# Regrouping gradients by a mask and four matmuls, and a shorter tail of the norm's backward, in a two-layer decode step with its backward

## The chip, the cores and the metric

The kernel runs on one core of a Trainium2 chip. The metric is the device time of one execution in microseconds; of several executions the median is given. Everything below is about one kernel before and one after the change.

## What is computed

Two layers, each an attention block over a long key and value cache and an MLP, with the gradients of the output with respect to all nine inputs. Cut to what matters:

```python
def _A_ref(x, k_cache, v_cache, wq, wo):          # x: 2 x 1 x 1024, caches: 2 x 4 x 16384 x 128
    q = (x @ wq).reshape(B, Sq, Hq, Dh)           # 32 heads of 128, 8 to each of 4 cached heads
    p = softmax(q @ k^T * Dh ** -0.5)
    return (p @ v) @ wo

def _B_ref(x, w1, b1, w2, b2):
    y = _layernorm(x, axis=-1)
    h = _gelu(y @ w1 + b1)                        # F = 3584
    return h @ w2 + b2

x = A_x
for layer in (0, 1):
    x = x + _A_ref(_layernorm(x), k_cache, v_cache, wq, wo)
    x = x + _B_ref(_layernorm(x), w1, b1, w2, b2) # _B_ref norms once more
out, vjp = jax.vjp(f, A_x, k_cache, v_cache, wq, wo, w1, b1, w2, b2)
grads = vjp(grad_out)                             # out and nine gradients are returned
```

There are two batch rows and a single query position, so every activation is a vector of 1024 (or 3584, or 4096) for each of two rows, while the caches and the weights are tens of megabytes that are read several times. The gradients of the caches and the weights are outer products of such vectors and are written in full.

## The kernel before

A vector lives in SBUF as a tile of 128 partitions by `DJ` = 8 columns by 2 batch rows (`[128, DJ, 2]`): element `j * 128 + p` stands in partition `p`, column `j`. The work goes through these stages: forward attention of layer 0, its MLP, forward attention of layer 1, its MLP together with the backward of that MLP, backward attention of layer 1 (`attn_bwd(1, ...)`), backward of layer 0's MLP, and backward attention of layer 0 (`attn_bwd(0, ...)`), in which nearly all gradients of weights and caches are also formed and written.

Every piece of work is a Python function handed to `emit`, with the chunks it uses. `Program.run` then walks the pieces in order; the order of instructions on each engine is the order of the pieces, and nothing is moved afterwards. Loads come from SyncE's queue into slots of 1 MB (`slot0` to `slot15` and parts of other tiles); a load is given a slot, and issued, as early as a slot is free whose use ends in time. In the last stage part of the slots becomes staging for outputs, which GpSimd's queue stores.

Two sides work on copies out of PSUM: `copy_bf` and `cast_out` choose between ScalarE and VectorE (DVE) by a running account of how busy each is, `st["act"]` and `st["dve"]`; pieces with fixed DVE work book it with `dve(...)`. PSUM banks for short uses come in rotation from `ob()`, three of them in most of the backward.

For weights that were only transposed in blocks of 32 (`turn_rows`, `turned_products`), a product comes out in what is called quad layout here: `acc[p, c, a, b]`, where partition block `p // 32` and the index `a` have changed places against the layout that the next step needs. `unquad` sets that right: DVE copies the PSUM region to the tile `uq`, and 16 copies of 32 partitions each move the blocks, dealt out to DVE, ScalarE and GpSimd in turn (lines L517, L525, L527, L529). It is used in seven places: `g3_` (gradient of layer 1's MLP input, `dm_1`), `g1p` (the same of layer 0, `dm_0`), three times in `wo_bwd_ops` (gradient of the attention's output in layer 0, `do_raw`, one for each cached head after the first, followed by `do_of`), `dh_last_` and `dn_kept`; the last two put all copies on GpSimd.

The backward of a norm is three helpers. `ln_bwd_terms` makes the two sums over columns (`lb_s`), `part_sum` sums them over partitions by a matmul with ones (L594), and `ln_bwd_rest` makes the gradient. Behind the partition sums these DVE operations follow one another: a scaling of the sums by -1/1024 (`lb_nm`, L665), for the MLP a second scaling (L667), three operations on `lb_u` (L669 to L671), the product with `rstd` (`lb_dx`, L673), the addition of the other gradient (L936 or L1191) and, where the next products need it, a cast to bf16 (L937 or L1194). `mlp_in_bwd` calls them for the MLP's input, `attn_in_bwd` for the attention's input; in `attn_in_bwd` the three parts `sums`, `close` and `rest` are pieces of their own.

`do_of` (L1002 to L1008) takes the regrouped gradient, spreads it for the next products (L563, L566) and sums it over partitions. `exchange` (L585) is the set of 16 copies, on ScalarE or GpSimd, that the backward attention needs for each half head. `kblock` transposes a block of a cache on DVE (L537) and uses it on TensorE (L550); `direct` (L575) uses it untransposed. L1266 and L1326 are the products of the outputs' gradients, L276 and L279 the casts of these to bf16 on ScalarE and DVE.

Of the kernel before, what the change touches and what calls it, by code (L numbers as in the profile page):

```python
# [182 lines left out]
def kernel(  # L183
# [113 lines left out]
    for w in range(2):  # L297
        for e in range(2):
            V.tensor_copy(out=selp[:, 2 * w + e],
                          in_=ident[:].rearrange("p (w t e) -> p w e t", w=2, e=2)[:, w, e].unsqueeze(1).to_broadcast(  # L300
                              [128, 4, 32]))
    neghalf = const.tile([128, 2], F32, name="neghalf")
# [349 lines left out]
    def ln_bwd_terms(dy, y):  # L652
        t1 = wrk.tile([128, DJ, 2], F32, name="lb_t1")
        V.tensor_tensor(out=t1[:], in0=dy, in1=y, op=ALU.mult)
        s = small.tile([128, 2, 2], F32, name="lb_s")
        V.tensor_reduce(out=s[:, 0, :], in_=dy.rearrange("p j b -> p b j"), axis=AX.X, op=ALU.add)
        V.tensor_reduce(out=s[:, 1, :], in_=t1[:].rearrange("p j b -> p b j"), axis=AX.X, op=ALU.add)
        return flat(s[:])

    def ln_bwd_sums(dy, y, at=None):  # L660
        return part_sum(ln_bwd_terms(dy, y), 4, at)

    def ln_bwd_rest(ps, dy, y, rstd, twice=False):
        nm = small.tile([128, 2, 2], F32, name="lb_nm")
        V.tensor_scalar(out=flat(nm[:]), in0=ps, scalar1=-1.0 / D, scalar2=None, op0=ALU.mult)  # L665
# [257 lines left out]
    def mlp_in_bwd(l, fill, gT, parts=False):  # L923
        h = {}

        def sums():
            y, _ = saved[f"m{l}"]
            h["dm"] = wrk.tile([128, DJ, 2], F32, name="dm_sb")
            fill(h["dm"])
            h["ps"] = ln_bwd_sums(h["dm"][:], y[:], half[0, 0] if parts else None)  # L930

        def rest():
            y, r = saved[f"m{l}"]
            dx = ln_bwd_rest(h["ps"], h["dm"][:], y[:], r[:], True)
            gn = vec.tile([128, DJ, 2], F32, name=f"gM{l}")
            V.tensor_tensor(out=gn[:], in0=dx[:], in1=gT[:], op=ALU.add)  # L936
            V.tensor_copy(out=gA_all[:, :, 2 * l:2 * l + 2], in_=gn[:])  # L937
# [23 lines left out]
    def wo_bwd_ops(l, k, vb):  # L961
# [3 lines left out]
        def fin():  # L965
            raw = small.tile([128, 8, 2], F32, name="do_raw")
            unquad(raw[:].rearrange("p (c j) b -> p c j b", j=4), acc)
            V.memset(sb[0][:, 64:80], 0.0)
            dve(1.1)
            do_of(l, k, raw[:])  # L970
# [200 lines left out]
    def attn_in_bwd(l, gT, dnq):  # L1171
        h = {}

        def sums():
            dn = wrk.tile([128, DJ, 2], F32, name="dn")
            last = sb[0][:, 112:128].rearrange("p (j b) -> p j b", b=2)
            if l == 1:
                V.tensor_copy(out=dn[:], in_=last)
            else:
                V.tensor_tensor(out=dn[:], in0=last, in1=dnq[:], op=ALU.add)  # L1180
            h["dn"] = dn
            h["s"] = ln_bwd_terms(dn[:], vec_y[f"a{l}"][:])
            dve(0.8)

        def close():
            h["ps"] = part_sum(h["s"], 4, half[0, 0] if l == 1 else sb[0][:, 200:])

        def rest():
            dx = ln_bwd_rest(h["ps"], h["dn"][:], vec_y[f"a{l}"][:], vec_r[f"a{l}"][:])
            gn = saved[f"gA{l}"]  # L1190
            V.tensor_tensor(out=gn[:], in0=dx[:], in1=gT()[:], op=ALU.add)  # L1191
            dve(1.3)
            if l == 1:
                V.tensor_copy(out=gM_all[:, :, 0:2], in_=gn[:])  # L1194
# [295 lines left out]
    def g3_():  # L1490
        saved["g3"] = mlp_in_bwd(1, lambda dm: unquad(dm[:].rearrange("p (c j) b -> p c j b", j=4), dm_1), gT4)
# [57 lines left out]
    g1p = mlp_in_bwd(0, lambda dm: unquad(dm[:].rearrange("p (c j) b -> p c j b", j=4), dm_0), g2, parts=True)  # L1549
# [97 lines left out]
```

## Time and profile before

| | us |
|---|---|
| median of 3 runs | 1108.54 |
| lowest and highest of them | 1106.45, 1108.61 |
| the profiled execution | 1104.69 |
| its span | 1102.9 |
| TensorE matmuls busy | 809.1 (73% of the span) |
| DVE busy | 759.6 (69%) |
| ScalarE busy | 492.6 (45%) |
| GpSimd busy | 181.7 (16%) |
| bytes moved by DMA | 448.98 MB, mean 407 GB/s |

The profile is of one execution. Engines are called PE (TensorE's matmuls), PEld (its weight loads), DVE, ACT (ScalarE), POOL (GpSimd) and SP (SyncE, which only issues DMAs here). A row of the timeline has the start in us from the span's start, the length in us, engine, line, operation, what it writes and reads, the form, the count and, in brackets, how long the engine had stood idle and what ended that. A row of the groups has busy us, mean ns of one, and idle us before. A row of the windows has the busy time and count of PE, PEld, DVE, ACT and POOL in a stretch, the clock granted to TensorE as a share of full speed, the DMA engines' mean busy share and the rate in GB/s. Idle time of an engine that does not bound a stage costs nothing.

### The profile page before, as it was taken

To read this page: it belongs to the slowest core of one execution; us is meant where nothing else is said; L and a number is where in the kernel's file an instruction comes from. 1 tells how busy PE (TensorE), PEld (TensorE's weight loads), DVE (VectorE), ACT (ScalarE), POOL (GpSimd) and SP (SyncE) were. 2 spreads that over 40 slices of the span, in tenths; PEclk is the share of its full clock that TensorE was granted. 3 is DMA by queue.
4 is the path that set the end of the run, shared out by engine and by line. 5 is a ranking of instruction groups with operands and counts; after the bars stand their busy time and mean duration, and the time that the engine had idled before them with its cause. 6 is when DMAs were issued, how large, how long until landed. Compare 5 with 4: busy or idle time off the path is not lost. (4 is left out here: it accounts for less than half of the span.)

```text
span 1102.9 us, 34164 instructions
## 1 busy us (share of the span) xinstructions
PE 809.1 (73%) x14665; PEld 607.6 (55%) x14677; DVE 759.6 (69%) x1472; ACT 492.6 (45%) x1133; POOL 181.7 (16%) x575
## 2 busy tenths in 40 slices
PE   5665666457788657688778678878876986598795
PEld 4554565456777556688778564444443443344453
DVE  5864665168888637755746466979876896598974
ACT  0332222101242321235534326767675776477874
POOL 1000000001000000111211101433332332233330
PEclk9999999999999999988978657989997999799998
DMA  9999999999999999999999998999999999999996
GB/s 372 420 423 421 421 425 423 397 385 413 416 422 421 422 420 383 419 418 421 416 421 419 389 413 307 366 400 424 419 420 425 423 419 422 425 411 420 411 423 269
DMA packets 97932, 448.98 MB, mean 407 GB/s; under 512 B 7624, under 2 KB 11742, under 8 KB 59380
## 3 DMA queue, kind: packets, MB, share of 16 engines
q1 hardware_dynamic: 80532, 351.32, 78.2%
q0 software_dynamic: 17248, 95.48, 21.0%
q8 instruction: 115, 1.88, 0.6%
q14 instruction: 37, 0.30, 0.1%
HBM read 348.15 MB, written 98.62 MB: 405 GB/s over the span
## 5 line engine op out<-in xcount | busy, mean ns | idle before, releaser
L537 DVE STREAM_TRANSPOSE kT<-slot 128x512 int32<-128x512 int32 x436 | 294.1, 695 | 109.5 <-PE sc L550 90.9
L550 PE MATMUL sc<-qbd,kT 128*128 128x32 bf16 x4096 | 263.0, 222 | 11.0 <-DVE kT L537 10.2
L550 PEld LDWEIGHTS <-kT 128*128 128x128 bf16 x4096 | 209.1, 115 | 65.3 <-issue 33.4
L575 PEld LDWEIGHTS <-slot 128*128 128x128 bf16 x3456 | 141.9, 103 | 101.4 <-issue 45.3
L575 PE MATMUL sb<-xt,slot 128*128 128x8 bf16 x3456 | 157.6, 177 | 45.7 <-DMA slot<-in_A_v_cache_dram 23.9
L276 ACT CAST slot<-sc 128x512 bf16<-128x512 f32 x281 | 160.8, 594 | 58.2 <-PE sc L1326 25.0
L1266 PE MATMUL sc<-slot,late 128*128 128x512 bf16 x344 | 127.8, 392 | 23.3 <-DVE slot L279 10.0
L279 DVE CAST slot<-sc 128x512 bf16<-128x512 f32 x172 | 115.2, 678 | 24.5 <-PE sc L1326 10.4
L768 ACT ACTIVATE e<-sc 128x512 bf16<-128x512 f32 x32 | 19.0, 597 | 234.8 <-DVE sc L765 168.6
L276 ACT CAST slot<-sb 128x512 bf16<-128x512 f32 x151 | 89.6, 593 | 37.0 <-PE sb L1326 25.3
L455 ACT COPY slot<-tp 128x512 int32<-128x512 int32 x88 | 50.4, 587 | 106.0 <-PE tp L452 90.3
L452 PE MATMUL tp<-ident,slot 128*128 128x128 bf16 x768 | 74.4, 260 | 11.0 <-DMA slot<-in_A_wq_dram 5.7
L585 ACT COPY xt<-e 32x128 int32<-32x128 int32 x256 | 75.6, 295 | 3.9
L1266 PEld LDWEIGHTS <-late 128*128 128x128 bf16 x512 | 44.5, 98 | 59.5 <-issue 45.7
L1266 PE MATMUL sb<-slot,late 128*128 128x512 bf16 x162 | 63.7, 393 | 7.6 <-DVE slot L279 1.9
L1326 PE MATMUL sc<-slot,late 128*128 128x512 bf16 x155 | 58.7, 401 | 13.8 <-DVE slot L279 9.9
L452 PEld LDWEIGHTS <-slot 128*128 128x128 bf16 x768 | 60.1, 119 | 13.6 <-issue 6.3
L437 DVE STREAM_TRANSPOSE slot<-slot 128x1024 int32<-128x1024 int32 (+1 forms) x46 | 52.9, 1178 | 18.6 <-DMA slot<-in_A_wo_dram 9.1
L279 DVE CAST slot<-sb 128x512 bf16<-128x512 f32 x80 | 54.1, 677 | 9.5 <-PE sb L1266 6.2
L645 POOL TENSOR_TENSOR m_rstd<-ln_vpe,neghalf 128x2 f32<-128x2 f32 x2 | 1.4, 719 | 349.0 <-DVE ln_vpe L643 349.0
L585 POOL COPY xt<-late 32x64 int32<-32x64 int32 x240 | 55.6, 232 | 13.0 <-DVE late L1054 1.9
L585 POOL COPY xt<-ds 32x64 int32<-32x64 int32 x128 | 29.7, 232 | 148.5 <-DVE ds L1054 113.9
(298 smaller groups left out, 1090.9 us busy)
## 6 DMA issues: line engine op xcount, KB each, us to landing
slot<-in_A_k_cache_dram SPq DMA_DIRECT2D x103, 1024.0 KB, 16.4
slot<-in_A_v_cache_dram SPq DMA_DIRECT2D x101, 1024.0 KB, 16.0
out_dram<-slot POOLq DMA_DIRECT2D x55, 1024.0 KB, 14.3
slot<-in_A_wq_dram SPq DMA_DIRECT2D x25, 1024.0 KB, 12.4
slot<-in_A_wo_dram SPq DMA_DIRECT2D x25, 1024.0 KB, 19.7
out_dram<-slot POOLq DMA_DIRECT2D x40, 512.0 KB, 14.1
slot<-in_B_w_dram SPq DMA_DIRECT2D x22, 896.0 KB, 16.4
slot<-in_B_w_dram SPq DMA_DIRECT2D x12, 1024.0 KB, 12.8
```

The costliest lines, as they stand in the source:

```text
L276: S.copy(out=dst, in_=src)
L279: V.tensor_copy(out=dst, in_=src)
L437: V.transpose(out=t.ap[:, h * nw * 256:(h + 1) * nw * 256].bitcast(I32).rearrange("p (w j m) -> p w j m", j=4, m=32), in_=c.ap[:, 0:4 * nc ...
L452: PE.transpose(tp[:, j * 128:(j + 1) * 128], c.ap[:, off + j * 128:off + (j + 1) * 128], ident[:])
L455: S.copy(out=d.bitcast(I32), in_=tp.bitcast(I32))
L537: V.transpose(out=kT[:].bitcast(I32).rearrange("p (w j m) -> p w j m", w=4, j=4), in_=c.ap[:, (i % 4) * 1024:(i % 4 + 1) * 1024].bitcast(I ...
L550: PE.matmul(sc[:, a0:a0 + 4, :, 2 * (i % 4) + q], lhsT=kv[:, 2 * q + w, :, e], rhs=qbd[:, q_at(g), 2 * w + e], start=(w == 0 and e == 0), ...
L575: PE.matmul(acc, lhsT=c.ap[:, n * 128:(n + 1) * 128], rhs=xv[:, i // 4, t // 2, :, 2 * (i % 4) + t % 2], start=(fresh and i == 0 and t == ...
L585: (GP.tensor_copy if on[t % len(on)] == "g" else S.copy)(out=d[32 * t:32 * t + 32, c0:c0 + cn, j, :], in_=s[32 * j:32 * j + 32, c0:c0 + cn ...
L768: S.activation(out=e_of(l, g)[:, 8 * f:8 * f + 8].rearrange("p a h b -> p h a b"), in_=sc[f][:].rearrange("p h (a b) -> p h a b", b=8), fu ...
L1266: PE.matmul(ps, lhsT=hold["blk"][:, j, :], rhs=flat(qm(w)[:, hf * 4:hf * 4 + 4, :]), start=True, stop=True)
L1326: PE.matmul(ps, lhsT=hold[j // 4 * 4][:, j % 4, :], rhs=Y.ap[:, y_at + c0:y_at + c0 + cn], start=True, stop=True)
```

## The change

`regroup` takes the place of `unquad` in `mlp_in_bwd` (both layers) and in `wo_bwd_ops`. It multiplies the PSUM region, with `a` spread over four columns, by a mask that keeps a partition's own block, and then sums blocks by four fp32 matmuls with a matrix of 128 x 32 ones at equal remainders; each writes 32 partitions of a PSUM bank. The result is read from PSUM by what follows; there is no copy to SBUF. `dh_last_` and `dn_kept` keep `unquad`.

In the norm's backward the product with `rstd` is made first, on the incoming gradient (`lb_dr`); the scalings go into the matrix of the partition sum (`mean`, -1/1024 in place of ones) and into the product in front of it; the other gradient is added to `lb_dr` between the partition sum's matmul and what reads it. Behind the sums stay a product, an addition and a last addition that is written directly, once for each form that is needed (bf16 for the products first, fp32 second). The account of DVE work is booked with 0.3 in place of 1.1 in the `do` step and 0.8 in place of 1.3 in `attn_in_bwd`.

```diff
+    quadT = vec.tile([128, 32], F32, name="quadT")
+    V.tensor_reduce(out=quadT[:], in_=identf[:].rearrange("p (a t) -> p t a", a=4), axis=AX.X, op=ALU.add)
+    mean = vec.tile([128, 1], F32, name="mean")
+    V.memset(mean[:], -1.0 / 1024)
+    meanf = mean[:].to_broadcast([128, 128])
...
+    def regroup(src, at):
+
+        C = src.shape[1]
+        q = small.tile([128, 8, 4, 2], F32, name="uq", bufs=1)[:, 0:4 * C]
+        V.tensor_tensor(out=q, in0=src.rearrange("p c a b -> p (c a) b").unsqueeze(2).to_broadcast([128, 4 * C, 4, 2]),
+                        in1=quad[:].unsqueeze(1).unsqueeze(3).to_broadcast([128, 4 * C, 4, 2]), op=ALU.mult)
+        ps = at[:, 0:8 * C].rearrange("p (c n) -> p c n", c=C)
+        qa = q.rearrange("p (c a) j b -> p c a (j b)", a=4)
+        for a in range(4):
+            PE.matmul(ps[32 * a:32 * a + 32], lhsT=quadT[:], rhs=qa[:, :, a], start=True, stop=True)
+        return ps.rearrange("p c (j b) -> p (c j) b", b=2)
...
-    def ln_bwd_terms(dy, y):
+    def ln_bwd_terms(dy, y, rstd, gT, twice=False):
+
+        dr = wrk.tile([128, DJ, 2], F32, name="lb_dr")
+        V.tensor_tensor(out=dr[:], in0=dy, in1=bcast_j(rstd, DJ), op=ALU.mult)
         t1 = wrk.tile([128, DJ, 2], F32, name="lb_t1")
-        V.tensor_tensor(out=t1[:], in0=dy, in1=y, op=ALU.mult)
+        V.scalar_tensor_tensor(out=t1[:], in0=dr[:], scalar=1.0 + LN_EPS if twice else 1.0, in1=y, op0=ALU.mult, op1=ALU.mult)
...
-    def ln_bwd_rest(ps, dy, y, rstd, twice=False):
-        nm = small.tile([128, 2, 2], F32, name="lb_nm")
-        V.tensor_scalar(out=flat(nm[:]), in0=ps, scalar1=-1.0 / D, scalar2=None, op0=ALU.mult)
-        if twice:
-            V.tensor_scalar(out=nm[:, 1, :], in0=nm[:, 1, :], scalar1=1.0 + LN_EPS, scalar2=None, op0=ALU.mult)
+        return dr, flat(s[:]), gT
+
+    def ln_bwd_sums(dr, s, gT, at=None):
+
+        ps = (ob() if at is None else at)[:, 0:4]
+        PE.matmul(ps, lhsT=meanf, rhs=s, start=True, stop=True)
+        V.tensor_tensor(out=dr[:], in0=dr[:], in1=gT, op=ALU.add)
+        return ps
+
+    def ln_bwd_rest(ps, dr, y, outs):
+
         u = wrk.tile([128, DJ, 2], F32, name="lb_u")
-        V.tensor_tensor(out=u[:], in0=y, in1=bcast_j(nm[:, 1, :], DJ), op=ALU.mult)
-        V.tensor_tensor(out=u[:], in0=u[:], in1=dy, op=ALU.add)
-        V.tensor_tensor(out=u[:], in0=u[:], in1=bcast_j(nm[:, 0, :], DJ), op=ALU.add)
-        dx = wrk.tile([128, DJ, 2], F32, name="lb_dx")
-        V.tensor_tensor(out=dx[:], in0=u[:], in1=bcast_j(rstd, DJ), op=ALU.mult)
-        return dx
+        V.tensor_tensor(out=u[:], in0=y, in1=bcast_j(ps[:, 2:4], DJ), op=ALU.mult)
+        V.tensor_tensor(out=u[:], in0=u[:], in1=dr[:], op=ALU.add)
+        for out in outs:
+            V.tensor_tensor(out=out, in0=u[:], in1=bcast_j(ps[:, 0:2], DJ), op=ALU.add)
...
         def sums():
-            y, _ = saved[f"m{l}"]
-            h["dm"] = wrk.tile([128, DJ, 2], F32, name="dm_sb")
-            fill(h["dm"])
-            h["ps"] = ln_bwd_sums(h["dm"][:], y[:], half[0, 0] if parts else None)
+            y, r = saved[f"m{l}"]
+            dm = regroup(src, half[0, 1] if parts else ob())
+            h["dr"], s, g = ln_bwd_terms(dm, y[:], r[:], gT[:], True)
+            h["ps"] = ln_bwd_sums(h["dr"], s, g, half[0, 0] if parts else None)
 
         def rest():
             y, r = saved[f"m{l}"]
-            dx = ln_bwd_rest(h["ps"], h["dm"][:], y[:], r[:], True)
             gn = vec.tile([128, DJ, 2], F32, name=f"gM{l}")
-            V.tensor_tensor(out=gn[:], in0=dx[:], in1=gT[:], op=ALU.add)
-            V.tensor_copy(out=gA_all[:, :, 2 * l:2 * l + 2], in_=gn[:])
+            ln_bwd_rest(h["ps"], h["dr"], y[:], [gA_all[:, :, 2 * l:2 * l + 2], gn[:]])
             return gn
...
         def fin():
-            raw = small.tile([128, 8, 2], F32, name="do_raw")
-            unquad(raw[:].rearrange("p (c j) b -> p c j b", j=4), acc)
+            raw = regroup(acc, ob())
             V.memset(sb[0][:, 64:80], 0.0)
-            dve(1.1)
-            do_of(l, k, raw[:])
+            dve(0.3)
+            do_of(l, k, raw)
...
         def close():
-            h["ps"] = part_sum(h["s"], 4, half[0, 0] if l == 1 else sb[0][:, 200:])
+            h["ps"] = ln_bwd_sums(h["dr"], h["s"], h["g"], half[0, 0] if l == 1 else sb[0][:, 200:])
 
         def rest():
-            dx = ln_bwd_rest(h["ps"], h["dn"][:], vec_y[f"a{l}"][:], vec_r[f"a{l}"][:])
             gn = saved[f"gA{l}"]
-            V.tensor_tensor(out=gn[:], in0=dx[:], in1=gT()[:], op=ALU.add)
-            dve(1.3)
-            if l == 1:
-                V.tensor_copy(out=gM_all[:, :, 0:2], in_=gn[:])
+            ln_bwd_rest(h["ps"], h["dr"], vec_y[f"a{l}"][:], ([gM_all[:, :, 0:2]] if l == 1 else []) + [gn[:]])
+            dve(0.8)
```

In `attn_in_bwd` the part `sums` calls `ln_bwd_terms` with `rstd` and the other gradient; in layer 1 it reads its input from PSUM where it was copied to SBUF before.

More of the change, by code (lines that the diff above doesn't have):

```diff
@@ L1174, in sums @@
         def sums():
-            dn = wrk.tile([128, DJ, 2], F32, name="dn")
             last = sb[0][:, 112:128].rearrange("p (j b) -> p j b", b=2)
-            if l == 1:
-                V.tensor_copy(out=dn[:], in_=last)
-            else:
+            if l == 0:
+                dn = wrk.tile([128, DJ, 2], F32, name="dn")
                 V.tensor_tensor(out=dn[:], in0=last, in1=dnq[:], op=ALU.add)
-            h["dn"] = dn
-            h["s"] = ln_bwd_terms(dn[:], vec_y[f"a{l}"][:])
+                last = dn[:]
+            h["dr"], h["s"], h["g"] = ln_bwd_terms(last, vec_y[f"a{l}"][:], vec_r[f"a{l}"][:], gT()[:])
             dve(0.8)
         def close():
-            h["ps"] = part_sum(h["s"], 4, half[0, 0] if l == 1 else sb[0][:, 200:])
+            h["ps"] = ln_bwd_sums(h["dr"], h["s"], h["g"], half[0, 0] if l == 1 else sb[0][:, 200:])
         def rest():
-            dx = ln_bwd_rest(h["ps"], h["dn"][:], vec_y[f"a{l}"][:], vec_r[f"a{l}"][:])
             gn = saved[f"gA{l}"]
-            V.tensor_tensor(out=gn[:], in0=dx[:], in1=gT()[:], op=ALU.add)
-            dve(1.3)
-            if l == 1:
-                V.tensor_copy(out=gM_all[:, :, 0:2], in_=gn[:])
+            ln_bwd_rest(h["ps"], h["dr"], vec_y[f"a{l}"][:], ([gM_all[:, :, 0:2]] if l == 1 else []) + [gn[:]])
+            dve(0.8)
         res = [(sums, ()), (close, ()), (rest, ())]
@@ L1490, in g3_ @@
     def g3_():
-        saved["g3"] = mlp_in_bwd(1, lambda dm: unquad(dm[:].rearrange("p (c j) b -> p c j b", j=4), dm_1), gT4)
+        saved["g3"] = mlp_in_bwd(1, dm_1, gT4)
     emit(g3_)
@@ L1548 @@
     va0, spread_a0 = spread(lambda: gA_all[:, :, 0:2], DJ, "va")
-    g1p = mlp_in_bwd(0, lambda dm: unquad(dm[:].rearrange("p (c j) b -> p c j b", j=4), dm_0), g2, parts=True)
+    g1p = mlp_in_bwd(0, dm_0, g2, parts=True)
     emit(g1p[0])
```

7 lines of the change are left out of this document (2 added, 5 removed).

## The prediction

> **What bounds the kernel now.** I read the page first, for the span and the slices, then the windows for the two places where the slices dip, then SyncE's timeline and the waits for what ends those dips, and last the timeline around each step that changes. The profiled execution took 1104.69 us; its span is
>
> ```profile
> span 1102.9 us, 34164 instructions
> GB/s 372 420 423 421 421 425 423 397 385 413 416 422 421 422 420 383 419 418 421 416 421 419 389 413 307 366 400 424 419 420 425 423 419 422 425 411 420 411 423 269
> ```
>
> so 1.8 us lie around it. The transfer rate stands near 420 GB/s almost everywhere and dips at slice 25 (662 to 689 us) and in the last one. The windows (columns: the five engines' busy time with counts, granted clock, DMA share, GB/s) say how deep:
>
> ```profile
> 677.00:680.00 3.00, 2.62 (x32) 1.34 (x31) 0.98 (x2) 3.00 (x8) 0.00 (x0) 1.00 0.01 3
> 680.00:683.00 3.00, 2.85 (x37) 1.60 (x34) 2.26 (x4) 3.00 (x9) 0.57 (x1) 1.00 0.45 49
> 683.00:686.00 3.00, 2.68 (x24) 1.08 (x22) 2.87 (x6) 2.38 (x6) 0.71 (x1) 1.00 0.92 328
> 730.00:1080.00 350.00, 283.06 (x3449) 153.99 (x3457) 276.41 (x476) 243.55 (x489) 118.74 (x349) 0.93 1.02 420
> 1080.00:1094.00 14.00, 10.49 (x107) 4.98 (x105) 10.61 (x26) 10.44 (x19) 2.15 (x4) 1.00 0.84 336
> ```
>
> From 730 to 1080 the DMA engines are never free (share 1.02, 420 GB/s); from 677 to 683 they stand still for 2.97 + 1.65 = 4.6 us; from 1080 to 1094 they are idle for 0.16 x 14 = 2.2 us (by the rates, 336 against 420, 2.8 us). Bytes do not change, so time can only be won where DMA idles. What ends the first dip is the issue of loads on SyncE:
>
> ```profile
> 659.42 0.38 SPq L378 DMA_DIRECT2D slot<-in_A_wo_dram  x1
> 669.31 0.33 SPq L373 DMA_DIRECT2D slot<-in_A_v_cache_dram  x1
> 680.98 0.33 SPq L373 DMA_DIRECT2D slot<-in_A_k_cache_dram  x1
> ```
>
> One load in 21 us: all slots are full until the last backward attention begins to use them up, and it begins behind the gradient step of layer 0's MLP (`g1p`). Before that, the compute waited on loads to the end of the second layer's backward attention:
>
> ```profile
> 635.42 0.93 PEld L575 LDWEIGHTS <-slot 128*128 128x128 bf16 x32 [3.55 <-DMA slot<-in_A_k_cache_dram]
> ```
>
> Here TensorE stood 3.55 us for a load. So whatever an earlier step wins (the first use of the new regrouping, `g3_`, stands ahead of that attention) is waited away by 635; I cost it at nothing, covered by that wait, and if the cover were gone it would bring about what the same step brings at 662, below. From 635 to the dip the chain is compute, and a microsecond won there is a microsecond less of idle DMA.
>
> **The change part by part.** I name the layers by their index, 1 and 0. Seven steps used `unquad`; five of them now regroup by a mask and matmuls (MLP gradients of both layers, three `do` steps of layer 0). The two with all copies on GpSimd stay.
>
> *The regrouping itself.* It replaces one copy and 16 small copies on three engines by a DVE product of 64 columns and four fp32 matmuls with 32 output rows. Nearest rows, the product first:
>
> ```profile
> L891 DVE TENSOR_TENSOR g_a<-hpre 128x56 f32<-128x56 f32 x2 | 0.4, 218 | 0.1
> ```
>
> 0.22 us, or 0.24 at 64 columns, and 0.06 to the next engine. For the matmuls no row has this form. An fp32 matmul shows as two weight loads and two matmuls, and the one of the MLP step in question, with 128 weight columns, stands so:
>
> ```profile
> 664.32 0.50 PEld L594 LDWEIGHTS sc<-lb_s,one 128*128 128x128 f32 x2 [2.68 <-DVE lb_s L657]
> 664.32 0.59 PE L594 MATMUL sc<-lb_s,one 128*128 128x4 f32 x2 [2.18 <-DVE lb_s L657]
> ...
> 664.95 0.16 DVE L665 TENSOR_SCALAR lb_nm<-sc 128x4 f32<-128x4 f32 x1 [0.68 <-PE sc L594]
> ```
>
> 0.63 us to its reader, 0.50 of it weight loads. Four such in series would be 2.5 us: the upper end. One of them is the lower end, 0.63. A weight load of few fp32 columns is shorter:
>
> ```profile
> L1370 PEld LDWEIGHTS sc<-identf,g_a 128*36 128x36 f32 x1 | 0.1, 97 | 0.6 <-DVE g_a L1368 0.6
> ```
>
> 97 ns at 36 columns, so eight of them 0.78 us and 0.13 us until the reader: 0.9 us, the value I take, since 36 columns are nearest to 32. With the product the regrouping takes 1.2 us (0.9 to 2.8).
> A row of the other narrow form, 64 output columns amid full ones, shows no gap around it:
>
> ```profile
> 673.13 0.64 PE L1247 MATMUL tp<-ident,e 128*64 128x128 bf16 x8
> ```
>
> The rule against the change is in the Trainium skill, "TensorEngine Tiling", Key Properties: changing the tiling mode drains TensorE, and four 32-column matmuls between full-width ones change it twice. By the row above the drain is invisible and the sum stays; if each drain cost one matmul's length of the fence before (0.59 / 2 = 0.3 us), each regrouping would take 0.6 us more and the forecast's gain would be 2.6 us in place of 3.2.
>
> *Layer 0's MLP step.* DVE alone, from the copy to the first operation of the norm's backward:
>
> ```profile
> 661.74 0.17 DVE L517 COPY uq<-sb 128x16 f32<-128x16 f32 x1 [1.49 <-PE sb L487]
> 661.95 1.03 DVE L525 COPY dm_sb<-uq 32x4 f32<-32x4 f32 x6
> 663.89 0.17 DVE L654 TENSOR_TENSOR lb_t<-dm_sb,m_y 128x16 f32<-128x16 f32 x1 [0.91 <-ACT dm_sb L527]
> ```
>
> 2.15 us, 0.91 of it a wait for ScalarE's share of the copies; 0.43 us later, at 664.32, the sums' matmul starts. After: 1.2 for the regrouping, one operation more in front of the sums (0.2), 0.43: 1.8 in place of 2.58, a gain of 0.7 us (a loss of 0.9 to a gain of 1.0). What is late next is not the norm's tail: behind the sums' matmul TensorE's queue holds six output matmuls, and only then the products that need the gradient, at
>
> ```profile
> 667.39 1.89 PE L465 MATMUL sb<-gA_all,slot 128*128 128x2 bf16 x64
> ```
>
> 2.4 us after the norm's first operation behind the sums (664.95); these six hide the shortened tail, so I count it at nothing here. The new wait: TensorE stands for DVE's product before the four matmuls, and queued behind it are these same six; they waited for the sums before, which came later.
>
> *Layer 1's attention norm, just before.* No regrouping, but the tail is on the path, since TensorE has nothing but the products behind it:
>
> ```profile
> 640.02 0.16 DVE L665 TENSOR_SCALAR lb_nm<-sc 128x4 f32<-128x4 f32 x1 [0.68 <-PE sc L594]
> ...
> 641.26 0.17 DVE L1194 CAST gM_all<-gA 128x16 bf16<-128x16 f32 x1
> ```
>
> Seven operations, 0.21 apart, end at 641.43: 1.41 us. Three remain (0.6): a gain of 0.8 us, 0.5 if each of the two that now read PSUM took 0.15 more. In front of the sums the count is unchanged (a copy goes, a product comes). The addition of the other gradient moves beside the sums' matmul (0.63) and is hidden by it.
>
> Together the dip ends 1.5 us earlier (a loss of 0.4 to a gain of 1.9).
>
> *The three `do` steps of layer 0.* The last of them:
>
> ```profile
> 953.13 0.17 DVE L517 COPY uq<-sb 128x16 f32<-128x16 f32 x1
> 953.33 1.14 DVE L525 COPY do_raw<-uq 32x4 f32<-32x4 f32 x6
> 954.48 0.07 DVE L968 MEMSET sb<- 128x16 f32 x1
> 957.04 0.17 DVE L1002 TENSOR_TENSOR dof<-do_raw,rbc 128x16 f32<-128x16 f32 x1 [2.50 <-POOL do_raw L529]
> ...
> 957.48 0.28 PE L563 MATMUL sb<-qd,selp 128*128 128x16 bf16 x4 [4.76 <-DVE qd L1003]
> ```
>
> 3.91 us, of which 2.50 waits for GpSimd, whose queue has `exchange` copies and a store's issue in front of its five copies. After: 1.2 us, a gain of 2.7 (1.1 to 3.0); GpSimd's store issues are no longer behind five copies. For the first two such steps I count nothing: DMA is saturated, and compute runs into late weights anyway:
>
> ```profile
> DVE slot L437 <- DMA slot<-in_A_wo_dram: 9.1, 2, 5.0
> ```
>
> (waits from 820 to 945). After 957 the only wait for a transfer is half a microsecond:
>
> ```profile
> DVE slot L279 <- DMA out_dram<-slot: 0.5, 1, 0.5
> ```
>
> So from the third step on compute runs free to the end, 2.7 us ahead; but it can win only what DMA idles in the last stretch, 2.2 us. I take 1.7, between nothing and all of it and nearer to the cap because the gain exceeds the cap; it is not all, because the last stores keep their own time from issue to landing. The final norm loses one DVE operation net (0.2 us), inside that.
>
> *The planner.* The new step books less DVE time, and in the built programs five casts of 512 columns go from ScalarE to DVE and four shorter copies the other way:
>
> ```profile
> L279 DVE CAST slot<-sc 128x512 bf16<-128x512 f32 x172 | 115.2, 678 | 24.5 <-PE sc L1326 10.4
> L525 DVE COPY do_raw<-uq 32x4 f32<-32x4 f32 x18 | 3.2, 178 | 0.3
> ```
>
> 5 x 0.678 = 3.4 us come, 3.2 us of small copies go, in the same stage: even. The order of loads on SyncE's queue is the same in both programs.
>
> Sum: 1.5 + 1.7 = 3.2 us; 1104.69 - 3.2 = 1101.5 for an execution like the profiled one. The median of the runs, 1108.54, lies 3.85 above it, so the forecast is 1108.54 - 3.2 = **1105.3**.
>
> **The rivals.** *Compute sets the end and the clock stays up.* In the do step TensorE stood 4.76 us, and behind it
>
> ```profile
> 957.00:963.00 6.00, 4.50 (x37) 2.42 (x39) 1.71 (x7) 3.34 (x7) 0.01 (x1) 0.50 1.02 426
> ```
>
> it worked 4.50 us at a granted clock of 0.50: at full clock 2.2 us less. If the shorter stand keeps the clock up and the last stores don't hold the end, the gain is 1.5 + 2.7 + 2.2 = 6.4 us, 1102.1. Against it: DMA's 1.02 share. The Trainium skill, "TensorE: Matmul & The Clock Gate", What's actually happening, has the clock halved after an idle window of about 3.4 us; the 4.76 us and the 0.50 agree.
>
> *Nothing that lasts.* The regrouping costs its upper 2.8 us, the MLP step loses 0.9 in place of winning, and the tail's idle is the stores' own: 0 to 2.2 us, about 1107.5. For it: no row has these matmuls.
>
> *Slower: weights behind stores.* Between the `do` steps compute runs faster, issues stores earlier, and these share the DMA engines with the weights and values that layer 0's steps at 922 to 941 us wait for. A store of 1 MB is 2.5 us at 420 GB/s. Three stores ahead delay the landing by 7.5; less 2.7 and 1.5 the end comes 3.3 us later, 1111.8. It decides from 6.4 us of delay on, two to three stores. For it: the waits of 5.0 us exist. Against it: stores ahead are also stores done.
>
> *The change does nothing of what it says:* the built program has one product and four matmuls in each of the five places and 80 copies fewer; no chance.
>
> **How the numbers follow.** A measurement tells about 0.2%, 2.2 us, from no change. Forecast 0.45 (its own range 1104.4 to 1106.3, wins of 2.2 to 4.1), the larger gain 0.13, nothing that lasts 0.25, slower 0.17: faster 0.58, same 0.25, slower 0.17. The range runs from 1101.0, below the larger gain, to 1110.0, over the second rival and the bounds of the runs; the third lies outside.
>
> **What would show it.** Right: in the changed profile the MLP step takes 1.8 us from the product to the sums' matmul; the load of 680.98 comes 1.5 us earlier and 677 to 683 idles about 3 us; DVE's wait for GpSimd in the `do` steps is gone, the product to `dof` takes 1.2 us, and 957 to 963 has a clock over 0.9. Wrong: four matmuls of over 2 us; an unchanged dip; longer waits for `wo` than 9.1 us; a last stretch that idles its 2.2 us as before.

## The result, and the profile after

| | before | after |
|---|---|---|
| median, us (22 runs each) | 1106.38 | 1104.51 |
| lowest, highest | 1105.24, 1109.65 | 1103.18, 1107.48 |
| profiled execution, us (span) | 1104.69 (1102.9) | 1103.3 (1101.5) |

The ratio after to before is 0.9981 (95% interval 0.9974 to 0.9988): 2.1 us less, between 1.3 and 2.9. The forecast was 3.2 less.

The changed kernel's windows (the same columns as before: five engines' busy time with counts, granted clock, DMA share, GB/s):

```profile
677.00:680.00 3.00, 2.88 (x39) 1.77 (x37) 1.42 (x2) 3.00 (x8) 0.40 (x1) 0.94 0.03 11
680.00:683.00 3.00, 2.70 (x24) 1.21 (x23) 2.61 (x5) 2.76 (x6) 0.51 (x2) 1.00 0.74 164
730.00:1080.00 350.00, 288.17 (x3463) 154.67 (x3462) 275.65 (x459) 240.00 (x475) 115.90 (x334) 0.92 1.01 421
1080.00:1094.00 14.00, 9.40 (x96) 4.39 (x94) 9.61 (x23) 8.97 (x16) 2.18 (x4) 0.99 0.79 310
957.00:963.00 6.00, 5.95 (x42) 2.43 (x41) 4.55 (x7) 3.48 (x8) 1.27 (x2) 0.69 1.02 429
```

From 677 to 683 DMA idles 2.9 + 0.8 = 3.7 us where it idled 4.6. From 1080 to 1094 it idles 0.21 x 14 = 2.9 us where it idled 2.2: no gain at the end. SyncE's timeline says when the loads around the dip are issued:

```profile
659.66 0.38 SPq L383 DMA_DIRECT2D slot<-in_A_wo_dram  x1
668.26 0.33 SPq L378 DMA_DIRECT2D slot<-in_A_v_cache_dram  x1
679.70 0.33 SPq L378 DMA_DIRECT2D slot<-in_A_k_cache_dram  x1
```

The load of 680.98 comes at 679.70. The MLP step of layer 0, in the changed kernel's timeline:

```profile
661.98 0.22 DVE L540 TENSOR_TENSOR uq<-sb,quad 128x64 f32<-128x64 f32 x1 [1.49 <-PE sb L492]
662.32 0.31 PE L545 MATMUL sc<-uq,quadT 128*32 128x16 f32 x8
662.69 0.18 DVE L672 TENSOR_TENSOR lb_dr<-sc,m_rstd 128x16 f32<-128x16 f32 x1 [0.49 <-PE sc L545]
663.34 0.59 PE L683 MATMUL sc<-lb_s,mean 128*128 128x4 f32 x2 [0.71 <-DVE lb_s L677]
664.38 0.17 DVE L693 TENSOR_TENSOR gA_all<-lb_u,sc 128x16 bf16<-128x16 f32 x1
666.40 1.83 PE L470 MATMUL sb<-gA_all,slot 128*128 128x2 bf16 x64
```

The regrouping takes 0.71 us to its reader, the step 1.36 us to the sums' matmul. The third `do` step, DVE's product to `dof`, takes 0.59 us, where it took 3.91:

```profile
951.79 0.21 DVE L540 TENSOR_TENSOR uq<-sb,quad 128x64 f32<-128x64 f32 x1
952.06 0.26 PE L545 MATMUL sb<-uq,quadT 128*32 128x16 f32 x8
952.38 0.17 DVE L1018 TENSOR_TENSOR dof<-sb,rbc 128x16 f32<-128x16 f32 x1 [0.23 <-PE sb L545]
```

Behind it, from 957 us on, stand waits for transfers, the longest of them below, that the kernel before did not have (it waited 0.5 us):

```profile
POOL out_dram L1287 <- DMA out_dram<-slot: 9.7, 2, 6.5
ACT e L276 <- DMA out_dram<-e: 4.5, 1, 4.5
DVE e L279 <- DMA out_dram<-e: 2.4, 1, 2.4
```

Layer 1's attention norm: the products that need its result start earlier behind the norm, and stop in mid-batch until the same time. The last K load's wait and the two parts of the batch, first of the changed kernel:

```profile
635.66 0.93 PEld L592 LDWEIGHTS <-slot 128*128 128x128 bf16 x32 [2.31 <-DMA slot<-in_A_k_cache_dram]
640.88 5.76 PE L470 MATMUL sb<-gM_all,slot 128*128 128x2 bf16 x211 [0.67 <-DVE gM_all L693]
649.17 0.49 PE L470 MATMUL sb<-gM_all,slot 128*128 128x2 bf16 x13 [2.52 <-issue]
```

and of the kernel before:

```profile
641.49 5.98 PE L465 MATMUL sb<-gM_all,slot 128*128 128x2 bf16 x219 [1.51 <-DVE gM_all L1194]
649.15 0.27 PE L465 MATMUL sb<-gM_all,slot 128*128 128x2 bf16 x5 [1.68 <-issue]
```

The batch has 224 products. TensorE stands 1.68 us in one kernel and 2.52 in the other, "issue" being time in which it waited for nothing that the profile shows, and goes on at 649.15 and 649.17.

### The profile page after: what moved, and what is told of

Read it like the earlier page. It is cut to its first block, busy times and chain, and to the rows that moved or that the text cites. A ratio compares the mean times of both kernels' runs of the same rounds, so it can differ in the third digit from the quotient of the medians.

```text
span 1101.5 us, 34179 instructions
## 1 busy us (share of the span) xinstructions
PE 814.9 (74%) x14717; PEld 608.0 (55%) x14717; DVE 756.1 (69%) x1438; ACT 486.1 (44%) x1107; POOL 177.0 (16%) x550
## 3 DMA queue, kind: packets, MB, share of 16 engines
q8 instruction: 115, 1.88, 0.6%
## 5 line engine op out<-in xcount | busy, mean ns | idle before, releaser
L276 ACT CAST slot<-sc 128x512 bf16<-128x512 f32 x288 | 163.9, 593 | 78.9 <-PE sc L1337 43.5
L1277 PE MATMUL sc<-slot,late 128*128 128x512 bf16 x338 | 127.4, 398 | 29.8 <-DVE slot L279 13.4
L279 DVE CAST slot<-sc 128x512 bf16<-128x512 f32 x168 | 112.8, 678 | 25.1 <-PE sc L1277 13.1
L276 ACT CAST slot<-sb 128x512 bf16<-128x512 f32 x137 | 81.1, 592 | 22.3 <-PE sb L1337 9.6
L1277 PEld LDWEIGHTS <-late 128*128 128x128 bf16 x512 | 44.9, 99 | 64.4 <-issue 51.7
L457 PE MATMUL tp<-ident,slot 128*128 128x128 bf16 x768 | 71.4, 253 | 9.5 <-DMA slot<-in_A_wq_dram 5.2
L1337 PE MATMUL sc<-slot,late 128*128 128x512 bf16 x169 | 65.7, 407 | 16.3 <-DVE slot L279 8.4
L1277 PE MATMUL sb<-slot,late 128*128 128x512 bf16 x174 | 69.7, 400 | 9.6 <-DVE slot L279 4.2
L279 DVE CAST slot<-sb 128x512 bf16<-128x512 f32 x91 | 61.8, 679 | 14.1 <-PE sb L1277 6.9
L602 POOL COPY xt<-ds 32x64 int32<-32x64 int32 x128 | 29.7, 232 | 176.8 <-DVE ds L1070 107.4
## 6 DMA issues: line engine op xcount, KB each, us to landing
slot<-in_B_w_dram SPq DMA_DIRECT2D x22, 896.0 KB, 16.6
```

The costliest lines, as they stand in the source:

```text
L276: S.copy(out=dst, in_=src)
L279: V.tensor_copy(out=dst, in_=src)
L457: PE.transpose(tp[:, j * 128:(j + 1) * 128], c.ap[:, off + j * 128:off + (j + 1) * 128], ident[:])
L602: (GP.tensor_copy if on[t % len(on)] == "g" else S.copy)(out=d[32 * t:32 * t + 32, c0:c0 + cn, j, :], in_=s[32 * j:32 * j + 32, c0:c0 + cn ...
L1277: PE.matmul(ps, lhsT=hold["blk"][:, j, :], rhs=flat(qm(w)[:, hf * 4:hf * 4 + 4, :]), start=True, stop=True)
L1337: PE.matmul(ps, lhsT=hold[j // 4 * 4][:, j % 4, :], rhs=Y.ap[:, y_at + c0:y_at + c0 + cn], start=True, stop=True)
```

## The experiments

The edits below are cut to the lines that matter. The profiled executions take 653 to 658 us to move the first 60 in 100 of their bytes, also where their programs are alike to there, so I compare stretches. The first table is worked out from the transfers' records of each profiled execution: the time between the moments at which 60, 65, 80 and 98 in 100 of its 449 MB had been moved, and the end of the last transfer. The dip lies between 60 and 65.

| kernel | to 60 | 60 to 65 | 65 to 80 | 80 to 98 | 98 to end | 80 to end |
|---|---|---|---|---|---|---|
| before | 653.5 | 64.4 | 160.9 | 193.2 | 29.4 | 222.6 |
| norm_only | 654.0 | 64.4 | 160.8 | 193.3 | 29.5 | 222.8 |
| regroup_do | 658.5 | 64.3 | 160.9 | 191.9 | 31.5 | 223.4 |
| after | 653.9 | 62.9 | 160.6 | 192.0 | 30.5 | 222.5 |
| regroup_only | 655.9 | 63.2 | 160.8 | 192.1 | 30.7 | 222.8 |
| regroup_mlp | 655.2 | 63.3 | 160.9 | 194.1 | 29.4 | 223.5 |
| drag_norm1 | 653.8 | 63.5 | 160.8 | 192.0 | 31.5 | 223.5 |
| shift128 | 657.0 | 63.0 | 160.6 | 192.4 | 30.8 | 223.2 |
| full92 | 657.4 | 63.2 | 160.7 | 192.9 | 29.7 | 222.6 |
| tail_half | 654.6 | 63.5 | 161.1 | 191.8 | 30.3 | 222.1 |
| drag_mlp0 | 656.2 | 66.6 | 160.8 | 191.8 | 31.0 | 222.8 |
| drag_do3 | 653.9 | 63.3 | 160.8 | 194.6 | 29.5 | 224.1 |
| fill0 | 655.5 | 66.4 | 160.6 | 193.3 | 30.5 | 223.8 |
| fill12 | 653.1 | 70.0 | 161.7 | 191.9 | 30.2 | 222.1 |

The second table takes from the timelines, in us behind the landing of the last K load (635.66 in the changed kernel): the start of the products on `gM_all`, after how many of 224 they break, how long TensorE stands, when it goes on, and the issue of the load that ends the dip.

| kernel | start | break after | stand | goes on | load |
|---|---|---|---|---|---|
| before | 6.07 | 219 | 1.68 | 13.73 | 45.56 |
| norm_only | 5.22 | 219 | 2.15 | 13.35 | 45.43 |
| regroup_do | 5.22 | 219 | 2.21 | 13.41 | 45.51 |
| after | 5.22 | 211 | 2.52 | 13.51 | 44.04 |
| regroup_only | 6.07 | 211 | 1.69 | 13.52 | 44.25 |
| regroup_mlp | 5.23 | 211 | 2.38 | 13.47 | 44.48 |
| drag_norm1 | 6.20 | 211 | 1.68 | 13.65 | 44.74 |
| shift128 | 5.23 | 147 | 1.98 | 11.27 | 43.77 |
| drag_mlp0 | 5.23 | 211 | 2.59 | 13.58 | 47.73 |
| fill0 | 5.22 | 211 | 2.47 | 13.46 | 43.69 |
| fill12 | 5.24 | 211 | 2.46 | 13.46 | 48.86 |

All ratios are to the kernel before; 0.001 is 1.1 us.

### The two halves of the change: norm_only, regroup_only

```diff
 # norm_only: regroup() made of the old copies
+    def regroup(src, at=None):
+        raw = small.tile([128, 8, 2], F32, name="do_raw")
+        unquad(raw[:].rearrange("p (c j) b -> p c j b", j=4), src)
+        return raw[:]
 # regroup_only: the kernel before, with the new regroup() in the five places
+            h["dm"] = regroup(src, half[0, 1] if parts else ob())
+            raw = regroup(acc, ob())
```

> The new norm's backward alone; the five regroupings are the old copies again. Theory (time is won only where the DMA engines idle, and layer 1's shorter tail is swallowed by TensorE's stall at 649 us, which ends when a page of its instructions has arrived): the stall ends at 649.1 to 649.2 us as in both kernels, layer 0's MLP step has one more operation before the sums and is 0.2 us longer than before, so the load that ends the dip comes at 681.0 to 681.2 us as before, and the time is that of the kernel before within 0.5 us (ratio 0.9995 to 1.0005). Rival (the norm's three operations win where they stand on the path, as I predicted): 0.8 us less than before, the load at 680.2.

> The regrouping by mask and matmuls alone, with the old norm's backward. Theory: the whole gain is here: layer 0's MLP step takes 2.58 - 1.4 = 1.2 us from the product to the sums' matmul, the load that ends the dip comes about 1.3 us earlier than 680.98, and the time is 2.1 us under the kernel before (ratio 0.998). Rival (norm and regrouping share it): 1.2 to 1.4 us under it, the remaining 0.8 us being the norm's.

Measured: norm_only 0.9995 (0.9986 to 1.0003), regroup_only 0.9985 (0.9975 to 0.9996). The dip's load stands at 45.43 and 44.25. The gain is the regrouping's; the norm's own part is no more than can be told from nothing. The norm-only batch did start 0.85 us earlier and go on 0.38 earlier (13.35), but its MLP step gave 0.2 back ahead of the sums.

### Where the regrouping pays: regroup_mlp, regroup_do

```diff
 # regroup_mlp: the copies stay in the three do steps
-            raw = regroup(acc, ob())
+            raw = copied(acc)
 # regroup_do: the copies stay in the two MLP steps
-            dm = regroup(src, half[0, 1] if parts else ob())
+            dm = copied(src)
```

> The changed kernel with the old copies in the three do steps; the regrouping stays in the two MLP steps. Theory (the whole gain is the dip's, the do steps give nothing that lasts): the dip's load at 44.0 us behind the K landing as in the changed kernel, the last 2 in 100 of the bytes in 29.5 us as in the kernels with copies there, and the time of the changed kernel (ratio 0.9977 to 0.9985). Rival (both places count): half of the gain, ratio 0.999.

> The changed kernel with the old copies in the two MLP steps and the regrouping in the three do steps alone. Theory (the do steps keep DMA from a short rest at 960 to 970 us, but most of it is given back at the end, where the last 2 in 100 of the bytes wait for compute): the dip's load at 45.4 us behind the K landing as in the kernel before, the time 0.3 to 0.9 us under the kernel before (ratio 0.9992 to 0.9997). Rival (my prediction's step, 1.7 us from the third do step): 1.7 us less than the kernel before, ratio 0.9985.

Measured: regroup_mlp 0.9986 (0.9977 to 0.9996), regroup_do 0.9999 (0.9988 to 1.0009). In the first table every kernel that regroups by matmuls in the MLP step and has nothing else changed there has 62.9 to 63.5 us from 60 to 65, each of the three that copy there 64.3 or 64.4. From 80 to the end it makes no difference whether the `do` steps copy (222.6, 222.8, 223.5) or regroup (222.1 to 223.5; fill0 and drag_do3, which change more than this, aside with 223.8 and 224.1). The prediction's 1.7 us from the third `do` step falls. The two columns before say how: the regrouping kernels reach 98 in 100 earlier (191.8 to 192.9, the same two aside; with copies 193.2 to 194.1) and take longer from there (29.7 to 31.5, with copies 29.4 or 29.5). No run regroups in one of the two MLP steps alone. That the gain is layer 0's rests on the second table, which counts from the last K load and so leaves out what layer 1's step won ahead of it, and on drag_mlp0 below.

### What a microsecond costs: drag_mlp0, drag_do3

```diff
+    drag = lambda t, n: [V.tensor_scalar(out=t, in0=t, scalar1=1.0, scalar2=None, op0=ALU.mult) for _ in range(n)]
 # drag_mlp0, in the sums of layer 0's MLP step
+            drag(s, 16 * parts)
 # drag_do3, in do_of, only the third do step of layer 0
+            drag(flat(dof[:]), 16)
```

> The changed kernel with 16 multiplications by one on DVE between the terms and the sums' matmul of layer 0's MLP step, about 16 x 0.16 = 2.6 us. Theory (this step is on the path that ends the dip, and every microsecond there is a microsecond of idle DMA): the load of 679.70 comes 2.6 us later and the time is 2.6 us over the changed kernel, 0.5 over the one before (ratio 1.0005). Rival 1 (TensorE is fed instructions at a fixed pace here, and what comes earlier waits for them): the load comes less than 1.3 us later and the time rises by less than 1.3. Rival 2 (the end is set by the saturated part and the last stores alone): the load moves, the time does not (ratio 0.998).

> The changed kernel with 16 such multiplications in layer 0's third do step, behind the first product, about 16 x 0.17 = 2.7 us: what the regrouping won there is given back. My prediction's step (compute runs free from there, of 2.7 us won 1.7 reach the end): 1.7 us over the changed kernel, so 0.4 us under the one before (ratio 0.9997). Theory now (behind 957 us stores and not compute hold the end, since the changed kernel waits 9.7 us for stores there where the one before waited 0.5): less than 0.5 us over the changed kernel (ratio 0.998 to 0.9985), and the waits for stores shrink by about 2.7 us.

The 16 operations took 3.2 us, not 2.6, as the row of drag_mlp0 shows (with the dip's load of that run):

```profile
665.81 3.23 DVE L535 TENSOR_SCALAR lb_s<-lb_s 128x4 f32<-128x4 f32 x16
...
685.82 0.33 SPq L378 DMA_DIRECT2D slot<-in_A_k_cache_dram  x1
```

drag_mlp0: 1.001 (1.000 to 1.002), that is 3.2 us over the changed kernel; the load comes 3.7 us later (47.73 against 44.04), and the stretch from 60 to 65 is 3.7 longer. One for one; both rivals fall. drag_do3: 0.9993 (0.9981 to 1.0005), 1.3 us over the changed kernel. The medians differ by less than their intervals, so this run alone doesn't decide between 0.5 and 1.7; its stretch from 80 to the end is the longest of all, 1.6 us over the changed kernel's, and its waits for stores shrink to 1.2 us. A step of 3.9 us (the copies) cost nothing there and one of 3.8 us on DVE alone some of its length: I have not settled the difference.

### Why the shorter norm of layer 1 brought nothing: drag_norm1, shift128

```diff
 # drag_norm1, in attn_in_bwd, layer 1
+            drag(flat(h["dr"][:]), 8 * l)
 # shift128, among the constants
+    [PE.matmul(obanks[0][0:32, 0:2], lhsT=ident[:, 0:32], rhs=ident[:, 0:2], start=True, stop=True) for _ in range(64)]
```

> The changed kernel with 8 multiplications by one on DVE in the tail of layer 1's attention norm, 8 x 0.20 = 1.6 us (0.20 as 16 of them took 3.23 us in layer 0's step). Theory (TensorE's stand at 649 us ends when a page of its instructions has come, 2.2 to 2.5 us after that transfer starts, whenever the products began): the products start 1.6 us later, the stand is shorter by about that (2.52 to 0.9), the products resume 13.3 to 13.7 us after the landing of the last K load as in the six kernels so far, the load that ends the dip stays 44.0 us behind that landing, and the time is that of the changed kernel (ratio 0.998). Rival (the page is asked for when TensorE gets so far, so that the stand moves along): resumed 15.1 us after the landing, the load 45.6, and 1.6 us more time (ratio 0.9995).

> The changed kernel with 64 small matmuls on the identity at the start of the program, where TensorE waits for its first load: 128 more instructions of TensorE ahead of everything, half a page of 256. Theory (the stand falls on a page's border in TensorE's stream of instructions): the first batch of products on gM_all breaks after 211 - 64 = 147 of 224 products, give or take 4, and not after 211. Rival (something of the program's data holds it there): it breaks after 211 again. On the time the theory says only that it moves by less than the stand's 2.5 us.

drag_norm1, ratio 0.9987 (0.9976 to 0.9998), which holds both expectations; the timeline tells them apart:

```profile
639.62 1.64 DVE L535 TENSOR_SCALAR lb_dr<-lb_dr 128x16 f32<-128x16 f32 x8
...
641.79 5.76 PE L470 MATMUL sb<-gM_all,slot 128*128 128x2 bf16 x211 [1.65 <-DVE gM_all L693]
649.24 0.48 PE L470 MATMUL sb<-gM_all,slot 128*128 128x2 bf16 x13 [1.68 <-issue]
```

The products start 0.98 us later (the rest of the 1.64 lies beside the sums' matmul), the stand shrinks from 2.52 to 1.68, and they go on 0.14 later. The load was 0.7 later, of which 0.6 arose behind the products that need layer 0's gradient, where kernels that are alike there differ by as much as 0.5. shift128, 0.9993 (0.9981 to 1.0005):

```profile
644.26 4.06 PE L470 MATMUL sb<-gM_all,slot 128*128 128x2 bf16 x147 [0.68 <-DVE gM_all L693]
650.30 2.19 PE L470 MATMUL sb<-gM_all,slot 128*128 128x2 bf16 x77 [1.98 <-issue]
```

The break moves from 211 to 147, by exactly the 64 products that 128 instructions are. The four fp32 matmuls of the first regrouping are 16 instructions, 8 products, and the break is after 219 in each kernel that copies there and, shift128 aside, 211 in the rest. Counted from the start, the same number of TensorE's matmuls and weight loads, 20417, stands ahead of the break in all fourteen traces. Every other stand of TensorE's matmuls over 0.9 us that the traces put down to "issue", 38 in the fourteen kernels, lies a multiple of 256 instructions from there, give or take one. So the stand hangs on a place in TensorE's stream of instructions, the border of a block of 256 (the expectations call such a block a page). The profile's page has the queue that brings them:

```profile
q8 instruction: 115, 1.88, 0.6%
```

115 transfers for 1.88 MB are 16 KB each, and TensorE's 14717 matmuls and 14717 weight loads in the changed kernel make 115.0 blocks of 256. In the changed kernel the transfers start at 640.69, 646.87 and 652.96; in all fourteen kernels the products go on 2.2 to 2.5 us after such a start. The Trainium skill, "Runtime: NRT & Kernel Launch", Instruction fetch mechanics, has blocks of 16 KiB, 256 instructions, fetched by DMA; the halfway shift agrees. It calls the cost of a crossing mostly hidden; with DMA at a share of 1.04 from 630 to 660 us it is 1.7 to 2.6 us here. What sets the start of the transfer is not shown.

### Trying to shorten the dip further: fill0, fill12

```diff
 # fill0
-    for u in first[9:15]:
-        emit(*u)
-    early = rest_h[:28] + ...
+    early = first[9:15] + rest_h[:28] + ...
 # fill12
-    for u in first[9:15]:
+    for u in first[9:21]:
```

> The changed kernel, with the six output matmuls that stand between the sums' matmul and the rest of layer 0's MLP step moved behind it, to the front of the list of outputs that later steps take from. Theory (only idle DMA counts): the load that ends the dip comes about 1.8 us earlier behind the K landing (44.04 to 42.2), but three half-full pieces of outputs, 0.75 MB or 1.9 us of transfer, are missing ahead of the dip, so the idle time stays and so does the time (ratio 0.9975 to 0.9985). Rival (the path to the load counts by itself): 1.8 us less than the changed kernel, ratio 0.9965.

> The changed kernel with 12 output matmuls in place of 6 between the sums' matmul and the rest of layer 0's MLP step, six of them taken from the list of later outputs: the opposite of the run that took all six away and was 3.9 us slower. Theory (only idle DMA counts, and outputs written ahead of the dip fill it): the load that ends the dip comes 1.8 us later, 0.75 MB more or 1.9 us of transfer go ahead of it, the idle time in the dip stays at 3.7 us or falls, and the time is that of the changed kernel or up to 2 us less (ratio 0.9965 to 0.998). Rival (the path to the load counts by itself): 1.8 us more, ratio 0.9997.

Both lose: fill0 1.0016 (1.0002 to 1.003), fill12 1.0056 (1.004 to 1.0073). In fill0 the products on `gA_all` come 1.7 us earlier as expected and the load 0.35, but DMA runs dry earlier, and stays short to 730 us (the last row shows 700 to 710):

```profile
674.00:677.00 3.00, 2.71 (x23) 1.39 (x23) 1.66 (x4) 2.53 (x6) 0.00 (x0) 0.62 0.49 206
677.00:680.00 3.00, 2.83 (x37) 1.50 (x35) 1.04 (x2) 3.00 (x8) 0.15 (x1) 1.00 0.00 0
...
700.00:710.00 10.00, 9.13 (x78) 4.55 (x77) 8.08 (x14) 6.77 (x14) 0.90 (x2) 0.83 0.87 294
```

(the changed kernel has shares of 0.87 and 0.03 in the first two windows, 0.74 from 680 to 683 and 0.98 from 700 to 710; with 0.73 from 680 to 683 in fill0, the idle time from 674 to 683 is 5.3 us against 4.1). I had expected no change and it was 3.9 us over the changed kernel: the dip idles 1.2 us more, and the rest was lost up to 730 us and at the end, under the new order of the outputs, which I have not taken apart. In fill12 the path grew by 3.6 us up to the products, not 1.8, because the norm's tail stood on DVE behind a cast that waited for TensorE:

```profile
667.98 0.69 DVE L279 CAST slot<-sc 128x512 bf16<-128x512 f32 x1 [5.24 <-PE sc L1337]
668.59 0.16 DVE L690 TENSOR_TENSOR lb_u<-m_y,sc 128x16 f32<-128x16 f32 x1
```

The load came 4.8 us later and the bytes ahead of it paid for none of that: the time is 8.3 us over the changed kernel. Part of the rest lies behind the dip, where DMA's share from 700 to 710 is 0.54 against 0.98; I have not taken that apart. No version here beats the changed kernel.

### What holds the end: full92, tail_half

```diff
 # full92
-FULL_AT = (4, 8, 12, 16)
+FULL_AT = (4, 8, 12, 16, 92)
 # tail_half, in dw_units, last piece of the wq gradient
-                    ps = ob()[:, 0:cn]
+                    ps = None if half_of and n % 2 else ob()[:, 0:cn]
```

> The changed kernel with one of the load buffers given over to outputs from step 92 of layer 0's attention on (about 945 us), a fifth one beside the four that change over early. Theory (what the shorter do step wins at 957 us is lost because compute then waits for output buffers whose stores stand in a full queue): the 16.6 us of waits for stores after 957 us shrink to less than half, the last 2 in 100 of the bytes take 29.5 us or less in place of 30.5, and the time is 1 to 2 us less than that of the changed kernel (ratio 0.9965 to 0.9975). Rival (those waits cost nothing; the end is set by the last gradient's chain and its stores): the waits shrink and the time stays (ratio 0.998). Against both: with a buffer less, loads come later and compute waits for them; then it is slower.

> The changed kernel without 8 of the 16 output matmuls of the last piece of the wq gradient and their 8 casts; all stores stay, and half of that piece is stale. Nothing before about 1083 us differs. Theory (from 80 in 100 of the bytes on, the stretch is as long as DMA needs plus the work behind the last loads, which no earlier gain of compute shortens; so this work itself shortens it): from 1083 to 1091 us DVE and ScalarE are both busy with casts of 0.68 and 0.59 us, 8 casts fewer are about 2.5 us less on each, and the time is 1.5 to 2.5 us under that of the changed kernel (ratio 0.996 to 0.997). Rival (the end is set by the transfers that stand in the queue at 1080 us and by the last stores' landing): the last store is issued 2.5 us earlier and the time stays within 0.5 us (ratio 0.998).

full92: 0.9984 (0.9975 to 0.9993), no better than the changed kernel. The waits for stores fell from 16.6 us to 3.2, and waits for loads took their place:

```profile
POOL out_dram L1287 <- DMA out_dram<-slot: 3.2, 1, 3.2
PEld L592 <- DMA slot<-in_A_k_cache_dram: 2.9, 1, 2.9
PE sb L592 <- DMA slot<-in_A_k_cache_dram: 2.7, 1, 2.7
```

So the rival held and the waits were not the cause: compute that is ahead of a full DMA waits for one thing or another. tail_half, which leaves out half of that piece's products and casts: 0.9987 (0.9977 to 0.9997), no faster either, but it did not test what I meant it to. In its profiled execution the clock was down while the casts were fewer:

```profile
1080.00:1085.00 5.00, 5.00 (x78) 3.13 (x76) 2.18 (x4) 2.18 (x3) 0.00 (x0) 0.50 0.69 283
1085.00:1090.00 5.00, 4.57 (x15) 1.80 (x15) 3.49 (x14) 3.62 (x7) 2.16 (x4) 0.59 0.65 258
```

(0.98 and 1.00 in the changed kernel), and the last stores, on SyncE, began no earlier behind the last store of `e` (17.6 us against 17.1). What holds the last 20 us stays open.

## Why the prediction was right, and where it was not

The bound was right: time was won where DMA idles and only there, in the dip. The forecast of 1105.3 lies 0.8 over the measured 1104.51, but part of that is luck: it was made from a median of 1108.54 of three runs, and the kernel's median over 22 is 1106.38. From there the forecast gain of 3.2 gives 1103.2. The gain was 1.1 too large: the measured 2.1 lies just under the 2.2 at which the forecast's own range of wins began, so that the time fell into that range is luck too. The dip's 1.5 alone is inside the measured interval of 1.3 to 2.9.

*The dip, 1.5 us:* right in sum, 64.4 - 62.9 = 1.5 from 60 to 65, and the load 1.52 earlier behind the K landing. The kernels alike in this stretch have 62.9 to 63.5, so 1.5 is the good end of 0.9 to 1.5. Its terms were off both ways. The MLP step begins 26.3 us behind the landing before and after, and the products on `gA_all` start at 31.96 and 30.75: 1.21 of the 1.52 arose in this step, nothing ahead of it, and 0.31 behind those products, within the 0.5 by which like kernels differ there. The regrouping, taken at 1.2 us, measured 0.71, under the lower bound of 0.9: I put eight weight loads in a row, and eight matmul records of about 0.2 us each end within 0.31, so they overlap; the reader starts 0.38 us after the first weight load. The Trainium skill, "TensorE: Matmul & The Clock Gate", The mechanism, has 32x32 tiles at different positions of the array hold weights of their own, write output slices of their own and overlap; the trace agrees. No drain shows on the way into the narrow mode: in the third `do` step they start at 952.06, as the full-width matmuls ahead of them end, and the reader stands 0.32 us behind. On the way back TensorE waits for DVE at all five places, which would hide one. So the MLP step took 1.36 in place of 1.8, a gain of 1.2 where 0.7 was booked. The norm of layer 1, booked at 0.8, gave the products 0.85 us, of which 0.22 were left where they go on and nothing at the MLP step: what was late next was a block of instructions, and my statement that TensorE "has nothing but the products behind it" did not ask whether it had them to execute. That the six output matmuls hide the tail of the MLP's norm held: `gA_all` is written at 664.38, used at 666.40.

*The first use, `g3_`, at nothing:* fits; TensorE still waits 2.31 us for the last K load, in place of 3.55.

*The last stretch, 1.7 us:* the step that failed. The third `do` step shrank by 3.3 us, more than the 2.7 booked, and the wait for GpSimd went. But "from the third step on compute runs free to the end" was wrong: 80 to the end took 222.5 in place of 222.6. The absence of waits in the kernel before meant that compute was just behind DMA, not that it could run ahead; once ahead, it waited 16.6 us for stores. And idle DMA after 1080 was not time that an earlier start could fill: the whole gain on the way to 98 in 100 was given back behind it.

*The first two `do` steps and the planner at nothing:* 65 to 80 took 160.6 in place of 160.9; held.

*What was to show it:* 677 to 683 idled 3.7 us, not about 3; the clock from 957 to 963 was 0.69, not over 0.9; and the last stretch idled as before, which I had named as a sign against.

*The rivals.* The larger gain didn't come, though that clock rose from 0.50: DMA's share there was 1.02 either way. Its condition failed too, since the shorter stand did not keep the clock up. In the changed kernel TensorE's longest stand from 943 to 960 us is 0.85 us, yet the granted clock is 0.50 from 953.9 to 960.7, and a product of 512 columns takes 0.38 us at 951.45, 0.59 at 954.36 and 0.38 again at 960.84. So a stand as long as the prediction's 4.76 us was not needed for it; what halved the clock there is not shown. "Nothing that lasts" was right for the last stretch, by another way than mine. Weights behind stores: the wait for `wo` fell from 9.1 to 6.9 us, that for `wq` rose from 3.4 to 6.6, and neither 65 to 80 nor 80 to the end grew.

## What to carry to other kernels

Cost a gain by the stretch it lies in: where DMA is saturated, a compute step that gets 3 us shorter turns into a wait for a store or a load, even if the profile before shows no such wait. A microsecond on the path to the load that ends a DMA gap was worth about a microsecond, in both directions, as long as the order of the work stayed: moving work off that path (fill0) made it 1.7 us shorter and the kernel slower. Before booking a shorter step, look at what the engine behind it does next to the end of its batch, "issue" stands included.

## What the runs showed of the hardware that I had not expected

TensorE stood 1.7 to 2.6 us in mid-batch in every one of the fourteen kernels, at a fixed place in its stream of instructions (20417 ahead of it in each), until 2.2 to 2.5 us after the start of a transfer of 16 KB on the instruction queue. Four fp32 matmuls of 32 output columns each, on four column groups, took 0.26 to 0.32 us together, from the first weight load to the last end, though a record of one is about 0.2 us. The granted clock fell to half for 6.8 us though TensorE had stood for at most 0.85 us in the 10 us before.
